# Moving the loads of q, k and v from SyncE's queue to GpSimd's in a fused attention and feed-forward kernel

## The chip, the cores and the metric

The kernel runs on one core of a Trainium2 chip. Five engines work side by side: TensorE (PE; its weight loads are shown as PEld), VectorE (DVE), ScalarE (ACT), GpSimd (POOL) and SyncE (SP), which computes nothing and only issues transfers and semaphores. Each engine runs its own instructions in order; transfers are carried out by 16 DMA engines. The metric is the time of one execution on the device in microseconds (us).

## The reference

For 8 batches of 8 heads, 576 tokens and 64 features (everything float32):

```python
scores = scale * np.matmul(q, k.transpose(0, 1, 3, 2))          # scale = 1/8
thresh = np.max(scores, axis=-1, keepdims=True) - tau            # tau = 0.02
scores = np.where(scores >= thresh, scores, -1000000000.0)
attn = np.exp(scores - np.max(scores, axis=-1, keepdims=True))
attn = attn / (np.sum(attn, axis=-1, keepdims=True) + 1e-09)
x = np.matmul(attn, v)            # heads side by side: 4608 tokens x 512
h = x @ w_in                      # 512 x 2048
out = np.maximum(0.01 * h, h) @ w_out                            # 2048 x 512
```

A weight of the attention is kept only where its score lies within `tau` of the row's largest.

## The kernel before

The work is cut into 72 **periods**: 128 queries of one batch by four heads (64 periods), and for each pair of batches two periods for the last 64 tokens of all heads (8 periods). A pair of batches makes 18 periods. A Python loop over `n` writes out all instructions in the order in which each engine is to run them; no scheduler moves them. Iteration `n` holds the scores of period `n`, the transposed transfer of the weights of period `n - 1`, the product with v of period `n - 2` (`PV_LAG = 2`), and a share of the feed-forward layers for groups of 128 tokens whose attention is done.

In one iteration the engines run, each in this order:

- PE: the score matmuls (L296) into one PSUM tile `sc` for four tiles of 128x576; transposes of the split q and k (`turn(keys)`, L186); a transpose that spreads the reciprocals (L401); four calls of `layer2` (L470), two of `layer1` (L457), and between them `pv` (L417), the weights times v. `l1q` holds what `layer1` is still to do. In odd iterations its second call takes the `x` that DVE has just written in the same iteration.
- DVE: copies of `sc` to SBUF with the row minimum (L332, four times; between the first two, half of the transposed q or k, L249), the reciprocals of the period before (L376), the thresholds `th` (L347: 128x4 values, SBUF to SBUF), `x` out of `pv` (L436), and the weights of three tiles (`weights`, L369: compare with the threshold, multiply, sum).
- ACT: three exponentials (`exp_plain`, L358), the leaky relu (L460), `by` (L407), every second period the output tile `osb` (L478), and `exp_steep` (L363, L364), which makes the weights of the fourth tile on ACT alone with a Prelu and an Exp.
- POOL: splits of q or k into a high and a low half (L160, L167, L171) ahead of their transposes, casts of v (L113, L119), one widening copy for each batch's keys (`widen_keys`, L253), and a one-instruction score signal (L325). The first work of POOL in an iteration waits for DVE's last weights of the period before (`behind_masks`). In iterations 0 to 2 POOL also issues the loads of `w_in` and `w_out` (L123, L127), four of 512 KB each.
- SP: `turn_w` (L380), one DMA that transposes the weights `w` of the period before into `wT`; then that iteration's loads of q, k and v; then the stores of finished output tiles.

The score signal orders two halves of the score matmuls that share a PSUM bank: it waits for a matmul of one row half, and the first matmul of the piece `a12` of the other row half waits for it. It sits on ACT for periods 0 to 2 and on POOL after that.

Loads are given to iterations by a table, `loads_at`. A main load of q, k or v (`load_main` L75, `load_v` L99) has 512 KB for four heads; tails (L93, L106) come as two transfers of 64 rows each. The first two batches' q and k are loaded in part by `load_part` (L86, 128 KB). From iteration 5 on, most iterations issue one to four loads; the last are issued in iteration 60. A load is used two or more periods after its issue.

SP's part of an iteration in the code:

```python
        elif before and st:
            turn_w(before)
        landed = [f() for f in loads_at.get(n, [])]
        while stores:
            store()
```

and the signal:

```python
            if (h, x) == (1, b12) and i == 2:
                signal = (nc.scalar if st.n < 3 else nc.gpsimd).nop()
```

The last group of tokens, (B-1, 3), is evacuated by ACT and DVE together (L475, L476) and stored by two queues (L492).

Of the kernel before, what the change touches and what calls it, by code (L numbers as in the profile page):

```python
# [12 lines left out]
AF = mybir.ActivationFunctionType  # L13
# [20 lines left out]
def kernel(  # L34
# [10 lines left out]
    nc = tc.nc  # L45
# [21 lines left out]
    raws, tails, vraws, vtails = {}, {}, {}, {}  # L67
    SRC = {"q": q, "k": k}

    def load_main(b, s, which):  # L70
        if (b, s, which) in MIXED:
            return [load_part(b, s, which, t=t) for t in range(4)][0]
        t = sb.tile([128, 4, 256], FP32, tag="raw", bufs=4, name="raw")
        raws[b, s, which] = t
        return nc.sync.dma_start(  # L75
            out=t[:, :, :], in_=SRC[which][b, ds(4 * s, 4), 0:MAIN, :].rearrange("h (p t) d -> p h (t d)", t=4))


# [2 lines left out]
    def load_part(b, s, which, h=None, t=None, eng=None):  # L81
        if (b, s, which) not in raws:
            raws[b, s, which] = sb.tile([128, 4, 4, 64], FP32, tag="raw", bufs=4, name="raw")
        src = SRC[which][b, ds(4 * s, 4), 0:MAIN, :].rearrange("h (p t) d -> p h t d", t=4)
        dst = raws[b, s, which]
        return (eng or nc.sync).dma_start(out=dst[:, :, h, :] if t is None else dst[:, t, :, :],  # L86
                                          in_=src[:, h, :, :] if t is None else src[:, :, t, :])

    def load_tails(b, which, engines=None):
        t = sb.tile([128, 2, 2, 64], FP32, tag="rawt", bufs=4, name="rawt")  # L90
        src = SRC[which][b, :, MAIN:S, :].rearrange("(u sh) p d -> u p sh d", u=2)
        for u, eng in enumerate(engines or (nc.sync, nc.sync)):
            eng.dma_start(out=t[ds(64 * u, 64), :, :, :].rearrange("p s h d -> p (s h) d"), in_=src[u])  # L93
        tails[b, which] = t

    def load_v(b, s):
        t = sb.tile([128, 4, 256], FP32, tag="vraw", bufs=2, name="vraw")
        vraws[b, s] = t
        return nc.sync.dma_start(  # L99
            out=t[:, :, :], in_=v[b, ds(4 * s, 4), 0:MAIN, :].rearrange("h (p t) d -> p h (t d)", t=4))  # L100

    def load_vtails(b):
        t = sb.tile([128, NP, 64], FP32, tag="vrawt", bufs=1, name="vrawt")
        src = v[b, :, MAIN:S, :].rearrange("(r h) p d -> h p r d", h=2)
        for h in range(2):
            nc.sync.dma_start(out=t[ds(64 * h, 64), :, :], in_=src[h])  # L106
        vtails[b] = t

    def cast_v(b, p, copy=None):
# [191 lines left out]
    def scores(st):  # L301

        st.mn = sb.tile([128, 4], FP32, tag="mn", bufs=2, name="mn")
        st.th = sb.tile([128, 4], FP32, tag="th", bufs=2, name="th")
        st.s, st.e = {}, {}
        (a00, a01), (b01, b00) = pieces(0, 0), pieces(0, 1)
        (a11, a12), (b12, b11) = pieces(1, 0), pieces(1, 1)
        todo = [[(0, a00), (0, a01), (1, a11), (1, a12)], [(1, b12), (1, b11), (0, b01), (0, b00)]]
        if st.n < 2:

            todo[1] = todo[1][2:] + todo[1][:2]
        todo = [[(c, x, i) for c, x in row for i in range(3)] for row in todo]
        at_, signal, first = [0, 0], None, None
        while todo[0] or todo[1]:
            h = 1 if not todo[0] or (todo[1] and at_[1] < at_[0]) else 0
            c, x, i = todo[h].pop(0)
            at_[h] += x[1]
            for mm in product(st, c, h, x, i):
                if first is not None:
                    tc.declare_no_dep(mm.ins, first.ins, reason="other banks")  # L320
                if (h, x) == (0, a12) and i == 0:
                    tc.add_manual_dep(mm.ins, signal.ins.name, BEHIND, reason="the row halves share a bank")
                last = mm
            if (h, x) == (1, b12) and i == 2:
                signal = (nc.scalar if st.n < 3 else nc.gpsimd).nop()  # L325
                tc.add_manual_dep(signal.ins, last.ins.name, BEHIND, reason="the row halves share a bank")
            if (h, x) == (0, a11) and i == 2:
                first = copy_min(st, 0)
# [135 lines left out]
    def layer2():  # L464
        g, r = l2q.pop(0)
        if r == 0:
            g.o = ps.tile([128, 512], FP32, tag="o", bufs=1, name="o")
        for j in (2 * r, 2 * r + 1):
            for c in range(2):
                nc.tensor.matmul(out=g.o[ds(64 * c, 64), :], lhsT=g.g[:, j, ds(64 * c, 64)],  # L470
                                 rhs=w_out16[:, j, :], start=(j == 0), stop=(j == 15), skip_group_check=True)
        if r == 7:
            g.out = sb.tile([128, 512], FP32, tag="osb", bufs=3, name="osb")
            if g.where == (B - 1, 3):
                nc.scalar.activation(out=g.out[:, 0:256], in_=g.o[:, 0:256], func=AF.Copy, bias=0.0, scale=1.0)  # L475
                nc.vector.tensor_copy(out=g.out[:, 256:512], in_=g.o[:, 256:512])  # L476
            else:
                nc.scalar.activation(out=g.out[:, :], in_=g.o[:, :], func=AF.Copy, bias=0.0, scale=1.0)  # L478
            stores.append(g)

    def store():
        g = stores.pop(0)
        b, m = g.where
        if m is None:
            for u in range(2):
                nc.sync.dma_start(out=out[ds((b + u) * S + MAIN, 64), :], in_=g.out[ds(64 * u, 64), :])
        else:
            rows = out[ds(b * S, MAIN), :].rearrange("(p t) f -> p t f", t=4)
            parts = (nc.scalar, nc.sync) if g.where == (B - 1, 3) else (nc.sync,)
            for i, eng in enumerate(parts):  # L490
                f = ts(i, 512 // len(parts))
                eng.dma_start(out=rows[:, m, f], in_=g.out[:, f])  # L492


    loads_at, turns_at, early32, late32, split_at_, pool_at = {}, {}, {}, {}, {}, {}
# [119 lines left out]
    n = 0  # L615
    while n < N + PV_LAG or l1q or pending or l2q or stores:
        st = periods[n] if n < N else None
        before = periods[n - 1] if 1 <= n <= N else None
        due = periods[n - PV_LAG] if PV_LAG <= n < N + PV_LAG else None
        here = before and before.n < 3  # L620
        keys, now32, late = turns_at.get(n, []), early32.get(n, []), late32.get(n)


# [30 lines left out]
        for key in keys:  # L654
            if key[1:] == ("t", "k"):
                widen_keys(key[0])
        if n < 4:
            idle((16, 10, 8, 4)[n], spare("o"))
        if here:
# [2 lines left out]
                turn_w_here(before, 0, 8, o)  # L662
        elif before and st:
            turn_w(before)
        landed = [f() for f in loads_at.get(n, [])]
        while stores:
            store()
        if n == 0:
# [12 lines left out]
        for half in range(2):  # L681
            if half == 1 and n == 3:
                exp_steep(st, 3)
            for _ in range(2):
                if l2q:
                    layer2()
            if l1q:
                layer1()
            elif n >= N:
                settle()  # L690
            if half == 0:
                if st:
                    exp_plain(st, 1)
                    exp_plain(st, 2)
                if here:
                    take_w(before, 0, 8, o, on_act)
                if late:
                    turn32(late)
                    take_high(late)
                if n == N:  # L700

                    before.wt = sb.tile([128, 2, 9, 128], FP16, tag="wT", bufs=4, name="wT")
                    free = [(sc[:, ts(i, 512)].bitcast(FP16), 8 * i, m) for i, m in enumerate((8, 8, 2))]
                    for o, first, m in free:
                        turn_w_here(before, first, m, o)
                if due and n <= N:
                    if n != 3:
                        pv(due)
                    evacuate(due)
                if n == N:  # L710
                    a, *more = [take_w(before, first, m, o[:, 0 : 128 * m], on_dve if first else on_act)
                                for o, first, m in free]
                    for x in more:
                        tc.declare_no_dep(x.ins, a.ins, reason="other banks")
            elif st and n != 3:
                exp_steep(st, 3)
        if here:
            o = ps.tile([128, 512], FP16, tag="o", bufs=1, name="wp")
            turn_w_here(before, 8, 4, o)
        for i in range(3 if st else 0):  # L720
            weights(st, i)
            if late and i == 0:
                take_low(late)
            if here and i == 1:
                take_w(before, 8, 4, o, on_dve)
# [34 lines left out]
```

## Time and profile before

| | |
|---|---|
| median of 3 runs | 484.28 us (483.44 to 484.53) |
| the profiled execution | 484.76 us, its span 482.9 us |
| PE busy | 465.4 us, 96% of the span |
| DVE, ACT, POOL busy | 434.8, 418.4, 190.9 us |
| granted TensorE clock | 1.00 |
| HBM read, written | 36.70 MB, 9.44 MB |
| transposed transfers `wT<-w` on SP | 68; from issue to landing 4.5 / 6.2 / 9.4 us (least, median, most) |
| main loads on SP, issue to landing | 4.9 to 5.6 us |

The span runs from the first to the last instruction of the trace; the execution's time has 1.9 us around it. [...] The chain that ended last is made up of PE by 75% and of the transfers `wT<-w` by 12%.

### The profile page before, as it was taken

What the parts mean: (1) busy time and instruction counts of PE and PEld (TensorE: products, weight loads), DVE (VectorE), ACT (ScalarE), POOL (GpSimd) and SP (SyncE); (2) the same over time, 40 slices, a digit from 0 to 9 for tenths busy, and PEclk for the clock granted to TensorE, in tenths of its full rate; (3) what the DMA queues carried; (4) which work ended last, traced back from release to release, by engine and by line L of the source; (5) the groups of instructions that cost most, each with busy time, mean ns of one, the idle gap of its engine ahead of it and who ended that gap; (6) DMA issues with size and microseconds to landing.
All of it is one profiled execution on the core that took longest, in us unless ns stands there. A gap on an engine that the chain in (4) does not pass through costs nothing.

```text
span 482.9 us, 25246 instructions
## 1 busy us (share of the span) xinstructions
PE 465.4 (96%) x10858; PEld 378.9 (78%) x10858; DVE 434.8 (90%) x1315; ACT 418.4 (87%) x777; POOL 190.9 (40%) x313
## 2 busy tenths in 40 slices
PE   7779999999999999999999999999999999999996
PEld 5567788888887788888887788888878888777785
DVE  4999989999999999999999999999998999999940
ACT  3888889999998899998998999999998899988862
POOL 2544436543554444353454554353454444000000
PEclk9999999999999999999999999999999999999999
DMA  9999998898979989799989969898989988657851
GB/s 177 237 210 218 193 224 167 160 192 194 190 165 207 182 165 188 151 177 192 193 167 215 209 142 189 150 194 181 203 167 184 215 168 135 124 122 123 122 96 45
DMA packets 216480, 83.68 MB, mean 173 GB/s; under 512 B 186032, under 2 KB 211888, under 8 KB 216368
## 3 DMA queue, kind: packets, MB, share of 16 engines
q1 hardware_dynamic: 210672, 77.42, 83.2%
q0 software_dynamic: 4224, 4.19, 5.3%
q8 instruction: 85, 1.39, 1.2%
q10 hardware_dynamic: 1472, 0.46, 0.4%
q14 instruction: 27, 0.22, 0.1%
HBM read 36.70 MB, written 9.44 MB: 96 GB/s over the span
## 4 chain that ended last, share of the span: by engine, by line
PE 75%; DMA 13%; ACT 6%; DVE 2%; issue 2%; SPq 0%; POOL 0%; ACTq 0%; POOLq 0%; DVEq 0%
PE hp L457 22%; PE o L470 22%; PE sc L296 18%; DMA wT<-w 12%; PE pv L417 8%; PE tp L401 3%; PE tp L186 2%; ACT e L358 1%; DVE w L369 1%; ACT w L364 1%; DMA vrawt<-in_v_dram 1%; ACT s L363 1%; ACT wT L393 1%; DMA raw<-in_k_dram 1%; DVE s L332 1%
## 5 line engine op out<-in xcount | busy, mean ns | idle before, releaser
L332 DVE TENSOR_SCALAR_CACHE_REDUCE s<-sc 128x576 f32<-128x576 f32 x288 | 205.4, 753 | 15.9 <-PE sc L296 15.8
L457 PEld LDWEIGHTS <-win 128*64 128x64 f16 x4608 | 146.8, 110 | 29.1 <-issue 1.4
L369 DVE SCALAR_TENSOR_TENSOR w<-s,th,e 128x576 f16<-128x576 f32 x216 | 166.3, 816 | 0.2
L358 ACT ACTIVATE e<-s,mn 128x576 f16<-128x576 f32 x216 | 159.7, 778 | 0.0
L470 PE MATMUL o<-wout,g 128*64 128x512 f16 x1152 | 149.3, 379 | 0.5 <-issue 0.5
L457 PE MATMUL hp<-x,win 128*64 128x128 f16 x4096 | 136.7, 219 | 0.3 <-DVE kT L249 0.3
L460 ACT ACTIVATE g<-hp 128x512 f16<-128x512 f32 x144 | 86.2, 598 | 44.5 <-PE hp L457 44.5
L296 PE MATMUL sc<-kT,qT 64*128 64x384 f16 (+7 forms) x1920 | 119.6, 284 | 0.7 <-DVE kT L239 0.7
L296 PEld LDWEIGHTS <-qT 64*128 64x128 f16 (+1 forms) x1920 | 90.3, 97 | 16.4 <-issue 1.4
L160 POOL TENSOR_SCALAR scaled<-raw 128x512 f32<-128x512 f32 x53 | 32.8, 620 | 169.0 <-DVE w L369 158.5
L470 PEld LDWEIGHTS <-g 128*64 128x64 f16 x1152 | 58.9, 110 | 28.6 <-ACT g L460 0.3
L171 POOL TENSOR_TENSOR half<-scaled,half 128x512 f16<-128x512 f32 (+1 forms) x68 | 71.8, 1056 | 5.8
L417 PE MATMUL pv<-wT,v 128*64 128x128 f16 (+1 forms) x1600 | 53.3, 215 | 4.9 <-DMA wT<-w 3.7
L364 ACT ACTIVATE w<-s,minus_tau 128x576 f16<-128x576 f32 x72 | 55.8, 775 | 2.3
L363 ACT ACTIVATE s<-s,th 128x576 f32<-128x576 f32 x72 | 55.2, 767 | 0.0
L417 PEld LDWEIGHTS <-v 128*64 128x64 f16 x1600 | 45.8, 110 | 6.6 <-PE hp L457 4.5
L167 POOL CAST half<-scaled 128x512 f16<-128x512 f32 (+1 forms) x68 | 38.4, 564 | 4.4
L436 DVE TENSOR_TENSOR x<-pv,by 128x256 f16<-128x256 f32 x64 | 27.1, 424 | 9.4 <-PE pv L417 5.7
L407 ACT COPY by<-tp 128x256 f16<-128x256 f16 x72 | 26.8, 372 | 3.4 <-PE tp L388 3.4
L186 PEld LDWEIGHTS <-half 64*128 64x128 f16 x968 | 24.4, 95 | 2.4 <-issue 1.5
L186 PE MATMUL tp<-ident,half 64*128 64x64 f16 x968 | 24.4, 190 | 0.0
L113 POOL CAST v<-vraw 128x256 f16<-128x256 f32 x64 | 24.1, 410 | 0.0
(58 smaller groups left out, 311.9 us busy)
## 6 DMA issues: line engine op xcount, KB each, us to landing
vraw<-in_v_dram SPq DMA_DIRECT2D x16, 512.0 KB, 5.2
out_dram<-osb SPq DMA_DIRECT2D x31, 256.0 KB, 5.0
raw<-in_q_dram SPq DMA_DIRECT2D x13, 512.0 KB, 5.6
raw<-in_k_dram SPq DMA_DIRECT2D x13, 512.0 KB, 4.9
win<-in_moe_w_in_dram POOLq DMA_DIRECT2D x4, 512.0 KB, 11.2
wout<-in_moe_w_out_dram POOLq DMA_DIRECT2D x4, 512.0 KB, 14.9
raw<-in_q_dram SPq DMA_DIRECT2D x12, 128.0 KB, 3.9
raw<-in_k_dram SPq DMA_DIRECT2D x10, 128.0 KB, 4.2
```

The source lines that it names most:

```text
L171: nc.gpsimd.tensor_tensor(out=halves[key][:, 1, 0:n, :, :], in0=scaled.pop(key)[:, 0:n, :, :], in1=halves[key][:, 0, 0:n, :, :], op=AX.sub ...
L186: nc.tensor.transpose(tps[key][r][:, x, t, :], half[rows, x, t, :, :].rearrange("p h d -> p (h d)"), ident[rows, rows])
L296: yield nc.tensor.matmul(out=o, lhsT=lhs, rhs=turned[st.b, "k"][rows, kx, pair, ds(key0, n)], start=(i == 0), stop=(i == 2), skip_group_ch ...
L332: return nc.vector.tensor_scalar(out=st.s[TILES[n]][:, :], in0=sc[:, ds(PLACE[TILES[n]], 576)], scalar1=-1.0 / UNIT, scalar2=None, op0=AX. ...
L358: nc.scalar.activation(out=st.e[t][:, :], in_=st.s[t][:, :], func=AF.Exp, bias=st.mn[:, n : n + 1], scale=-1.0)
L363: nc.scalar.activation(out=z, in_=z, func=AF.Prelu, bias=st.th[:, n : n + 1], scale=-1.0, alpha=1e20)
L364: nc.scalar.activation(out=w_of(st, t), in_=z, func=AF.Exp, bias=minus_tau[:, :], scale=1.0, accum_out=st.sum[:, c, h : h + 1])
L369: st.last = nc.vector.scalar_tensor_tensor(out=w_of(st, t), in0=st.s[t][:, :], scalar=st.th[:, n : n + 1], in1=st.e[t][:, :], op0=AX.is_le ...
L417: nc.tensor.matmul(out=st.pv[ds(64 * h, 64), c, ts(u, n)], lhsT=v16[st.b % 2][:, pair, blk, :], rhs=st.wt[:, c, blk - (blk > 4), ts(u, n)] ...
L457: nc.tensor.matmul(out=hp[ds(64 * c, 64), jj, :], lhsT=w_in16[:, i, ds(128 * (4 * u + jj) + 64 * c, 64)], rhs=g.x[:, i, :], start=(i == 0) ...
L460: nc.scalar.activation(out=g.g[:, ds(4 * u, 4), :], in_=hp[:, :, :], func=AF.Prelu, bias=0.0, scale=1.0, alpha=0.01)
L470: nc.tensor.matmul(out=g.o[ds(64 * c, 64), :], lhsT=g.g[:, j, ds(64 * c, 64)], rhs=w_out16[:, j, :], start=(j == 0), stop=(j == 15), skip_ ...
```

## The change

Four edits. From iteration 5 on, the loads of q, k and v are issued by GpSimd instead of SyncE, behind the splits, casts and widening copies of the iteration; before that they stay where they were. The score signal sits on ACT for periods 0 to 2, on POOL for 3 to 5 and on SP from 6 on. In period 1 the third tile is made by `exp_steep` on ACT like the fourth, so DVE makes the weights of two tiles and ACT runs one plain exponential less and one Prelu and Exp more. The last group is evacuated and stored by row halves (64 rows of 512 columns) instead of column halves, and the two copies are declared independent. The transfers' addresses and sizes are otherwise the same: 84 DMA instructions move from SP to POOL.

```diff
+    loader = [nc.sync]
+
     def load_main(b, s, which):
...
-        return nc.sync.dma_start(
+        return loader[0].dma_start(
...
     def load_part(b, s, which, h=None, t=None, eng=None):
...
-        return (eng or nc.sync).dma_start(out=dst[:, :, h, :] if t is None else dst[:, t, :, :],
+        return (eng or loader[0]).dma_start(out=dst[:, :, h, :] if t is None else dst[:, t, :, :],
...
     def load_tails(b, which, engines=None):
-        for u, eng in enumerate(engines or (nc.sync, nc.sync)):
+        for u, eng in enumerate(engines or (loader[0], loader[0])):
...
     def load_v(b, s):
-        return nc.sync.dma_start(
+        return loader[0].dma_start(
...
     def load_vtails(b):
-            nc.sync.dma_start(out=t[ds(64 * h, 64), :, :], in_=src[h])
+            loader[0].dma_start(out=t[ds(64 * h, 64), :, :], in_=src[h])
...
             if (h, x) == (1, b12) and i == 2:
-                signal = (nc.scalar if st.n < 3 else nc.gpsimd).nop()
+                signal = (nc.scalar if st.n < 3 else nc.gpsimd if st.n < 6 else nc.sync).nop()
...
             if g.where == (B - 1, 3):
-                nc.scalar.activation(out=g.out[:, 0:256], in_=g.o[:, 0:256], func=AF.Copy, bias=0.0, scale=1.0)
-                nc.vector.tensor_copy(out=g.out[:, 256:512], in_=g.o[:, 256:512])
+                a = nc.scalar.activation(out=g.out[0:64, :], in_=g.o[0:64, :], func=AF.Copy, bias=0.0, scale=1.0)
+                x = nc.vector.tensor_copy(out=g.out[64:128, :], in_=g.o[64:128, :])
+                tc.declare_no_dep(x.ins, a.ins, reason="other rows")
...
             for i, eng in enumerate(parts):
-                f = ts(i, 512 // len(parts))
-                eng.dma_start(out=rows[:, m, f], in_=g.out[:, f])
+                n = 128 // len(parts)
+                eng.dma_start(out=rows[ts(i, n), m, :], in_=g.out[ts(i, n), :])
...
+        plain = 2 if n == 1 else 3
...
             if key[1:] == ("t", "k"):
                 widen_keys(key[0])
+        if n >= 5:
+
+            loader[0] = nc.gpsimd
+            for f in loads_at.get(n, []):
+                f()
...
         elif before and st:
             turn_w(before)
-        landed = [f() for f in loads_at.get(n, [])]
+        if n < 5:
+            for f in loads_at.get(n, []):
+                f()
         while stores:
             store()
...
                 if st:
-                    exp_plain(st, 1)
-                    exp_plain(st, 2)
+                    for i in range(1, plain):
+                        exp_plain(st, i)
...
             elif st and n != 3:
-                exp_steep(st, 3)
+                for i in range(plain, 4):
+                    exp_steep(st, i)
...
-        for i in range(3 if st else 0):
+        for i in range(plain if st else 0):
             weights(st, i)
```

## The prediction

> **What bounds the kernel now.** I read the shares first, then the waits, then single periods.
>
> From part 1 of the page:
>
> ```profile
> PE 465.4 (96%) x10858; PEld 378.9 (78%) x10858; DVE 434.8 (90%) x1315; ACT 418.4 (87%) x777; POOL 190.9 (40%) x313
> ```
>
> PE (TensorE) works in 96% of the span, POOL (GpSimd) in 40%. The edit moves work off SP, which computes nothing, onto POOL, so the question is what PE still waits for. The list of waits (engine, its line, what it waited for: us in total, times, longest):
>
> ```profile
> DVE s L332 <- PE sc L296: 15.8, 62, 0.4
> ...
> PE pv L417 <- DMA wT<-w: 3.7, 7, 0.8
> ```
>
> The first row says that VectorE (DVE) has about 0.25 us to spare in a period. The second is the one large wait of PE that the moved queue can touch: seven times `pv` stood for the transposed weights. Two undisturbed periods and a stalled one, from the table of windows (stretch, length, busy us of each engine, granted clock, DMA share, GB/s):
>
> ```profile
> 102.93:109.04 6.11, 6.11 (x148) 5.01 (x145) 5.88 (x19) 5.85 (x11) 2.40 (x3) 1.00 0.99 211
> 109.04:115.15 6.11, 6.11 (x148) 5.02 (x144) 5.88 (x19) 5.47 (x10) 2.40 (x3) 1.00 0.81 164
> 145.77:152.60 6.83, 6.31 (x150) 5.20 (x146) 6.06 (x19) 5.47 (x10) 2.86 (x7) 1.00 1.02 219
> ```
>
> An undisturbed period is 6.11 us, all of it PE, with DVE 0.23 behind. The clock is at full speed, so it plays no part. Period 21 lost 0.72. [...]
>
> ```profile
> 140.36 0.55 SPq L99 DMA_DIRECT2D vraw<-in_v_dram  x1
> 140.96 0.49 SPq L492 DMA_DIRECT2D out_dram<-osb  x1
> 141.95 4.41 SPq L380 DMA_TRANSPOSE wT<-w  x1
> 146.41 0.58 SPq L75 DMA_DIRECT2D raw<-in_k_dram  x1
> 147.09 2.13 SPq L106 DMA_DIRECT2D vrawt<-in_v_dram  x2
> 149.38 3.26 SPq L380 DMA_TRANSPOSE wT<-w  x1
> ```
>
> The turn of 141.95 was issued 1.6 us behind a 512 KB load and 1 us behind a store; its issue took 4.41 and its data landed at 150.02, 8.07 later, with `pv` waiting. The three loads behind it (2.71) then kept SP until 149.22, so the next turn started 3.6 us after its period's scores instead of 2.29. The tile of these transfers shows how common that is:
>
> ```profile
> L380 SPq DMA_TRANSPOSE wT<-w x68: 2473/3183/5870, 38.5 to 458.2; - x68
> ...
> DMA to landing us min/median/max: 4.5/6.2/9.4
> ```
>
> `pv` needs the data some 7.5 us after issue: the median turn has 1.3 us to spare, and those issued right behind loads have nothing.
>
> **Turns without loads ahead of them: −2.9 us.** Stalled periods that the edit can reach are 21 (6.83), 23 (6.85), 33 (6.56), 39 (7.12) and 41 (6.79): above 6.11 that is 0.72 + 0.74 + 0.45 + 1.01 + 0.68 = 3.6, less 0.11 twice, since periods 22 and 40 then took 6.00: 3.4. In the quiet stretch without loads (iterations 63 to 70) turns land in 4.6 to 6.6, all in time. In the changed kernel loads leave POOL about 4.3 us after the scores begin, that is 2 us after the turn's issue and well before the next turn, and no turn queues behind them. A load can now run beside the end of the turn just issued, though. If it delayed that landing by 0.5 us, the parts above their slack over the 30 such turns sum to 0.5. I take −3.4 + 0.5 = −2.9 (ends −3.4 and 0).
>
> **Period 6: +0.8 us.** Turns of periods 3 and 4 lie behind transfers that the edit leaves (0.37 and 0.70 of wait in iterations 5 and 6). But four q loads of 128 KB, issued on SP at 51.45 when turn 4 was out, now leave POOL from about 48.7, beside that turn (issued 48.11, landed 54.97, needed at once). They hold 0.5 MB; at the 0.2 MB per us of the page's GB/s row that is 2.5 us of transfer. Ends 0 and +2.5; I take a third, since the first packets of a turn come 1.2 us after its issue and so lead those of the loads by about a microsecond.
>
> **What the loads cost on POOL.** No 512 KB load from POOL is in the steady part; the nearest rows are the weight loads, of the same size: 0.75 us for each. POOL has 3.5 us free in a period, so its own time costs nothing. But the weight loads show a neighbour that suffers:
>
> ```profile
> 26.33 1.49 POOL L127 DMA_DIRECT2D wout<-in_moe_w_out_dram  x2
> ```
>
> ```profile
> 27.25 0.17 DVE L376 RECIPROCAL rec<-sum 128x4 f16<-128x4 f32 x1
> 27.36 0.46 DVE L347 TENSOR_SCALAR th<-mn 128x4 f32<-128x4 f32 x1
> ```
>
> `th`, DVE's 128x4 threshold, has a median of 0.17 us. Here it took 0.46, ending with the second of the two POOL instructions, inside which it began by 0.29; at 19.76 it took 0.49 and began 0.26 inside. `rec` was not held. [...]
>
> Behind `th` on DVE stands `x` (L436), which `layer1` takes at once in odd iterations (0.05 to 0.15 us of slack); in even ones DVE's 0.23 of idle time takes back part. So the cost hangs on where the loads fall. The first operation of POOL in a period starts with DVE's last weights, and `th` comes 3.3 us later. POOL's work ahead of the loads takes 2.54 (one split: the load of 0.75 is just over), 3.0 to 3.1, 3.23 (split and two casts), or about 4 (behind `th`). Period 20 has the third kind, with 0.74 of casts there and `th` at their heels:
>
> ```profile
> 143.37 0.74 POOL L113 CAST v<-vraw 128x256 f16<-128x256 f32 x2
> ```
>
> ```profile
> 144.18 0.17 DVE L347 TENSOR_SCALAR th<-mn 128x4 f32<-128x4 f32 x1
> 144.26 0.42 DVE L436 TENSOR_TENSOR x<-pv,by 128x256 f16<-128x256 f32 x1
> ```
>
> The load would begin at about 144.11, `th` 0.07 later. The rows show `th` held when it came 0.26 into such an instruction, and none that came earlier. I let it pass under 0.2. Then it is held in odd periods 13, 21, 31, 39 and 49 by 0.23, 0.27, 0.22, 0.27, 0.22 = 1.2, less 0.05 of slack each: **+1.0** (ends +0.5 and +6.0, the upper one in the first rival).
>
> **Edits that cost little.** The score signal waits on SP behind the turn's issue: from 2.29 to 5.0 in a median period, up to 8.2 with the longest (the store adds 0.5); it is needed at 6.11 + 1.15 = 7.26. Behind it stands only the next turn, due later. Cover is the 2 us between; without it one period loses up to 1. I take 0. The third tile of period 1 takes 0.81 + 0.08 from DVE and puts 0.77 + 0.78 + 0.19 for one exp of 0.78 on ACT; iteration 5's `pv` waits for a turn landing at 47.91 whatever comes before: 0 (−0.15 to +0.3). At the end the osb copies ran one behind the other (ACT 0.38 at 479.09, DVE 0.42 at 479.51). Side by side, over half the rows and twice the columns, about 0.6 and 0.69: ready at 479.78 in place of 479.94: −0.15.
>
> **Sum.** −2.9 + 0.8 + 1.0 + 0 + 0 − 0.15 = −1.25, from 484.76 (the span of 482.9 and 1.9 around it) to 483.5. That run lay 0.48 above the median 484.28; on that scale: **483.0**. Its own range is 481.3 to 484.6.
>
> **Rival 1: the loads hold `th` (slower).** The deciding point is whether a POOL load holds `th` from its very start, as the widening copy L253 did: `th` began 13 ns behind it and took 0.63. Then the periods of 3.23 count in full. Odd ones: 7, 13, 17, 21, 31, 35, 39, 49, 53, 57, by 0.42 + 0.23 + 0.49 + 0.50 + 0.22 + 0.50 + 0.50 + 0.22 + 0.49 + 0.50 = 4.1, less 0.05 to 0.15 each; nine even ones (20, 22, 24, 26 and those 18 later, 58) hand on up to 0.27 each: 4.0 to 6.0, I take 4.5. −2.9 + 0.8 + 4.5 − 0.15 = +2.25: 486.5, up to 488. [...]
>
> **Rival 2: the load starves the turn beside it (slower).** Turn 3, issued at 38.51 while the weight loads of POOL's queue still ran, took 9.4 to land. If each load delays its own period's turn by 1.2 us, the parts above slack sum to about 4 in place of 0.5 (1.0 gives 2.2; 1.5 already 8.4): −3.4 + 4 + 0.8 + 1.0 − 0.15 = +2.25: 486.5, with a tail to 491. Against it: a load's first packets come 1 to 1.7 us after its start, when most of the turn is through.
>
> **Rival 3: the queue is not the cause.** The bytes stay the same, DMA share is 0.8 to 1 with loads, and if landings spread by that alone, turns stay as late: 0 + 0.8 + 1.0 − 0.15 = +1.65: 485.9. [...]
>
> **Chances.** Forecast 0.52 (0.08 of it ends within 0.2%), rival 1 0.22 (0.04 within), rival 2 0.16 (0.02), rival 3 0.10 (0.02). 0.2% is 1 us, about what a measurement of this kernel can tell from no change. Faster 0.44, same 0.16, slower 0.40. The range runs from the forecast's lower end to past rivals 1 and 3, leaving out the tail of rival 2: 481.2 to 489.0.
>
> **What would show it.** Right: turns landing within 7 us, the wait of `pv` for `wT` under 1.5 us in total, periods 21 to 41 at 6.11 to 6.3, a few `th` of 0.4 to 0.6. Rival 1: twenty or more long `th`, each with `hp` waiting behind `x` in odd periods. Rival 2: turn landings above 7.5 in periods with loads. Wrong altogether: PE waiting for the signal's semaphore, or splits waiting for late loads.

## Result and the profile after

The changed kernel took 510.96 us (median of 5 runs, 507.11 to 511.36) against 484.28 us: 1.054 times as long, with an interval of 1.049 to 1.058. The forecast was 483.0, its range 481.2 to 489.0, so both the sign and the range were wrong. The profiled execution has a span of 509.6 us, 26.7 more than before.

First the page of the changed kernel: busy time, then the DMA queues (packets, MB, share of the 16 engines' span).

```profile
PE 472.8 (93%) x10858; PEld 383.6 (75%) x10858; DVE 434.8 (85%) x1313; ACT 420.0 (82%) x779; POOL 246.7 (48%) x394
...
q1 hardware_dynamic: 178080, 54.87, 62.4%
q0 software_dynamic: 11024, 26.74, 21.6%
```

The loads went to the software queue as planned: q0 carries 26.74 MB, and POOL runs 81 instructions more (394 against 313), so 81 loads moved and not 84. VectorE works exactly as long as before, PE 7.4 us longer, and the span grew by 26.7: PE waits. The list of waits says for what (total us, times, longest):

```profile
PEld L419 <- issue: 19.0, 9, 5.6
PE pv L419 <- DMA wT<-w: 18.4, 10, 5.5
```

`pv` (L417, now L419) stood 18.4 us for the turn's data where it had stood 3.7. The row of PEld goes with the same stalls, seen from the weight loads, so the two are not added. The tile of the turns:

```profile
L382 SPq DMA_TRANSPOSE wT<-w x68: 2441/2953/7001, 38.2 to 484.3; - x68
...
DMA to landing us min/median/max: 4.6/6.6/14.3
```

The median turn is issued in less time (2.95 us against 3.18): SyncE did get shorter work, which is what the forecast counted on. But the data lands later (6.6 against 6.2), and the worst turn takes 14.3. Of 68 turns 21 took over 7.5 us, before 8. Set against the kernel before, period by period (from VectorE's first copy of one period to that of the next), 18.6 of the 26.7 us lie in three periods: 21 (+7.8), 39 (+6.0) and 57 (+4.8), 18 apart; 5 and 6 cost 3.1, and 16 has 1.9. The windows of period 21 and of two undisturbed ones (columns as before):

```profile
151.06:165.67 14.61, 8.66 (x149) 6.62 (x146) 7.20 (x22) 5.59 (x10) 4.45 (x10) 0.77 1.07 158
178.38:184.50 6.12, 6.12 (x149) 5.02 (x146) 5.81 (x19) 5.85 (x11) 4.75 (x8) 1.00 0.60 132
184.50:190.61 6.11, 6.11 (x149) 5.01 (x146) 5.88 (x19) 5.47 (x10) 4.62 (x8) 1.00 0.94 133
```

The undisturbed periods are still 6.11: nothing is lost where the turn is in time. Period 21 lasts 14.61, and the granted clock is 0.77 there. What led to it, on POOL's timeline and in the chain that ended last:

```profile
144.64 0.78 POOL L101 DMA_DIRECT2D vraw<-in_v_dram  x1
...
149.34 0.81 POOL L77 DMA_DIRECT2D raw<-in_k_dram  x1
150.16 1.24 POOL L108 DMA_DIRECT2D vrawt<-in_v_dram  x2
```

```profile
147.24 13.67 DMA wT<-w
160.91 0.14 issue
161.05 1.28 PE pv L419 x20
```

A load of v was issued 2.6 us ahead of the turn of 147.24, one of k 2.1 us behind it and two tails of v after that. That turn took 13.67 us. Ahead of it on SyncE's queue lay only a store of 144.37, which landed at 147.62; the four loads landed between 152.74 and 160.70, the turn at 160.91. In those 13.67 us the 16 engines carried 0.88 MB of SyncE's queue and 1.16 MB of GpSimd's side by side.

### The profile page after: what moved, and what is told of

It is laid out like the page before. It is cut to its first block, busy times and chain, and to the rows that moved or that the text cites. A ratio compares the mean times of both kernels' runs of the same rounds, so it can differ in the third digit from the quotient of the medians.

```text
span 509.6 us, 25224 instructions
## 1 busy us (share of the span) xinstructions
PE 472.8 (93%) x10858; PEld 383.6 (75%) x10858; DVE 434.8 (85%) x1313; ACT 420.0 (82%) x779; POOL 246.7 (48%) x394
## 3 DMA queue, kind: packets, MB, share of 16 engines
q0 software_dynamic: 11024, 26.74, 21.6%
## 4 chain that ended last, share of the span: by engine, by line
PE 70%; DMA 18%; ACT 6%; issue 2%; DVE 2%; SPq 0%; ACTq 0%; DVEq 0%
PE hp L459 20%; PE o L472 20%; DMA wT<-w 17%; PE sc L298 17%; PE pv L419 8%; PE tp L403 3%; PE tp L188 2%; ACT e L360 1%; ACT s L365 1%; ACT wT L395 1%; ACT w L366 1%; DMA raw<-in_k_dram 1%; DVE w L371 1%; DVE s L334 1%; ACT g L462 0%
## 5 line engine op out<-in xcount | busy, mean ns | idle before, releaser
L459 PEld LDWEIGHTS <-win 128*64 128x64 f16 x4608 | 149.5, 111 | 29.2 <-issue 1.9
L472 PE MATMUL o<-wout,g 128*64 128x512 f16 x1152 | 150.9, 383 | 0.0
L459 PE MATMUL hp<-x,win 128*64 128x128 f16 x4096 | 139.0, 221 | 0.3 <-DVE kT L251 0.3
L298 PE MATMUL sc<-kT,qT 64*128 64x384 f16 (+7 forms) x1920 | 120.8, 284 | 2.8 <-ACTq L327 1.1
L298 PEld LDWEIGHTS <-qT 64*128 64x128 f16 (+1 forms) x1920 | 90.3, 97 | 20.0 <-ACTq L327 2.0
L419 PE MATMUL pv<-wT,v 128*64 128x128 f16 (+1 forms) x1600 | 54.3, 217 | 22.4 <-DMA wT<-w 18.4
L419 PEld LDWEIGHTS <-v 128*64 128x64 f16 x1600 | 46.5, 112 | 24.9 <-issue 19.0
L334 DVE DVE_READ_ACCUMULATOR s<-sc 128x1 f32 x288 | 24.2, 84 | 0.0
```

What stands on the lines that cost most here:

```text
L298: yield nc.tensor.matmul(out=o, lhsT=lhs, rhs=turned[st.b, "k"][rows, kx, pair, ds(key0, n)], start=(i == 0), stop=(i == 2), skip_group_ch ...
L334: return nc.vector.tensor_scalar(out=st.s[TILES[n]][:, :], in0=sc[:, ds(PLACE[TILES[n]], 576)], scalar1=-1.0 / UNIT, scalar2=None, op0=AX. ...
L419: nc.tensor.matmul(out=st.pv[ds(64 * h, 64), c, ts(u, n)], lhsT=v16[st.b % 2][:, pair, blk, :], rhs=st.wt[:, c, blk - (blk > 4), ts(u, n)] ...
L459: nc.tensor.matmul(out=hp[ds(64 * c, 64), jj, :], lhsT=w_in16[:, i, ds(128 * (4 * u + jj) + 64 * c, 64)], rhs=g.x[:, i, :], start=(i == 0) ...
```

## Experiments

Times are medians, ratios stand against the kernel before in the same session (484.95, 485.05 and 485.58 us there). "Over" is the span of the profiled execution less the 482.9 of before. Single executions of one kernel spread by 3 to 7 us where the turns are disturbed, and single periods by several us from profile to profile. e8 to e12 and e14 ran once each.

**e1: loads back on SyncE, the rest of the change kept.**

```diff
-        if n >= 5:
-            loader[0] = nc.gpsimd
-            for f in loads_at.get(n, []):
-                f()
...
-        if n < 5:
-            for f in loads_at.get(n, []):
-                f()
+        for f in loads_at.get(n, []):
+            f()
```

> The changed kernel with one edit undone: the loads go back to SyncE, behind the turn; signal on SyncE, the third tile of period 1 and the row halves at the end stay. Theories of the 26.7 us: (Q) a load on a second queue shares the DMA engines with a turn and delays it; (S) the signal, now behind the turn's issue on SyncE, delays the scores. By Q the time comes back to 484 (483.5 to 485), turns land in 4.5/6.2/9.4 as before. By S at least 5 us stay: above 489.

500.75 us, ratio 1.030 (1.025 to 1.036), where Q had 484 and S above 489: here the signal decides. The turns did come back, as Q had it: four took over 7.5 us, and `pv` stood 2.6 us for them instead of 18.4. But the signal now stands behind loads on SyncE:

```profile
PEld L298 <- SPq L327: 18.2, 14, 3.0
...
PE sc L298 <- SPq L327: 14.0, 13, 2.7
```

PE stood 14.0 us for SyncE's signal (L327), up to 2.7 us at a time, of 16.2 over; the row of PEld has the same stalls from the weight loads. So the signal can stand on SyncE only if the loads do not; the two edits belong together, and in the changed kernel what it still costs is small: its rows there are

```profile
  ACTq L327: 3.1, 4
  SPq L327: 2.8, 5
```

under the scores (L298). These rows add PE and its weight loads: the 2.8 us on SyncE are three stalls, in two of which PE itself stood, 0.9 us in all. The ACT row belongs to periods 0 to 2.

**e2: the loads' queue alone.**

```diff
-    signal = (nc.scalar if st.n < 3 else nc.gpsimd if st.n < 6 else nc.sync).nop()
+    signal = (nc.scalar if st.n < 3 else nc.gpsimd).nop()
...
-        plain = 2 if n == 1 else 3
+        plain = 3
```

and the column halves at the end, as before.

> The kernel before with one edit alone: loads from period 5 on GpSimd's queue; the signal stays on GpSimd from period 3, now behind the loads. By Q the time is that of the changed kernel, 507 to 512, with the great stalls in periods 21, 39 and 57. By S it is under 500, since the signal no longer waits for a turn's issue.

504.55 us, ratio 1.041 (1.036 to 1.047); 20.3 over: above S's 500 and a little under Q's 507. No signal on SyncE, and three quarters of the loss are there; the other 6 us of the changed kernel no run takes apart. Period 6 lost 5.8, period 57 6.2, period 21 only 1.3: which turn is hit changes, that some are hit does not.

**e3 and e5: the same loads, released later.** POOL's loads wait for VectorE's first weights of the period; e5 also has the signal on POOL and period 1 and the end as before.

```diff
         for i in range(plain if st else 0):
             weights(st, i)
+            if i == 0 and n >= 5:
+                loader[0] = nc.gpsimd
+                for f in loads_at.get(n, []):
+                    for mm in f():
+                        behind_masks(mm, st)
```

> The changed kernel with the loads on GpSimd held until VectorE has made the first weights of the period, about 1.4 us later (5.8 us after the scores begin in place of 4.3), when most of the turn just issued is through and the next is 2.6 us off. If what hurts is that the loads leave too early, beside that turn (T), the time comes back to 484 to 488. If a load from this queue delays any turn that it meets (Q), it now meets the next one: 500 to 515.

490.91 us, ratio 1.012 (1.006 to 1.017): above T's 488, and far below Q's 500. So the loads do not simply delay the next turn in place of this one.

> As e3 (loads on GpSimd behind VectorE's first weights), but with the score signal back on GpSimd and period 1 and the end as before: of the change only the loads' queue is left, with the later release. e3 was 6.0 us over before in its profile; 0.7 of it at the end, some 5.9 where PE waited for the signal or a turn. If the release decides (T) and the signal was the rest, 484 to 487. If the queue itself costs (Q), 489 or more. A cost of its own: in iterations with three or four loads GpSimd issues until 7.9 to 8.3 us after the scores begin, and the next signal, due at 7.26, stands behind it: up to 1 us in each of some six periods.

487.52 us, ratio 1.007 (1.004 to 1.010), just above the band of T and below Q's 489. Same queue, same bytes, and 17 of the 20 us are gone. PE's first two rows of waits for e5:

```profile
PE pv L418 <- DMA wT<-w: 3.8, 5, 1.4
PE wp L389 <- ACT wT L394: 2.8, 3, 1.4
```

3.8 us for the turns is what the kernel before has (3.7). The feared wait for the signal behind the loads is there and is small: five stalls, 2.0 us for the weight loads and 0.5 for PE itself.

**e6: an intermediate release,** by VectorE's `x` instead of its first weights; otherwise e5.

```diff
                     evacuate(due)
+                    if n >= 5:
+                        loader[0] = nc.gpsimd
+                        for f in loads_at.get(n, []):
+                            for mm in f():
+                                tc.add_manual_dep(mm.ins, due.evacuated.ins.name, BEHIND, ...)
```

> As e5, but the loads are released by VectorE's x, 5.0 us after the scores begin: 0.7 us later than in the changed kernel, 0.8 us earlier than in e5. If the load does harm by meeting the turn just issued (T), it lies between e2 (20 us over) and e5, nearer to e5: 487 to 494, and the great stalls of periods 6, 21, 39, 57 are under 3 us. If the release plays no part, it is at e2's 503 to 506.

491.40 us (median of three executions; a fourth took 499.23), ratio 1.013 (1.010 to 1.017): between e2 and e5, as T has it, but the great stalls were not all under 3: periods 6 and 57 lost 5.2 and 4.3. Measured from the turn's issue to the load's (median of POOL's loads), the three releases give a row: 2.1 us, 504.6; 3.45 us, 491.4; 4.0 us, 487.5. The kernel before issues its loads 3.55 us behind the turn, on the turn's own queue, at 485.

**e4: a second hardware queue.** The loads from period 5 are issued by ScalarE.

```diff
                     for i in range(1, plain):
                         exp_plain(st, i)
+                        if i == 1 and n >= 5:
+                            loader[0] = nc.scalar
+                            for f in loads_at.get(n, []):
+                                f()
```

> The changed kernel with the loads from period 5 issued by ScalarE behind its second exponential: a second hardware queue in place of the software queue, at about the same time. Each issue takes ScalarE some 0.5 to 0.6 us. If any second queue delays the turns (Q), great stalls stay in periods 21, 39 and 57 and the time is 500 to 515. If it is the software queue with its packets of 4096 bytes (P: 159 ns each against 46 ns for 1024 on SyncE's queue), the turns land in under 8 us and the time is 484 to 492, what is lost being ScalarE's time.

504.81 us, ratio 1.043 (1.038 to 1.049). 20 turns took over 7.5 us, 21 in the changed kernel. This speaks for Q, but not cleanly: the loads left 1.7 us behind the turn, earlier than in e2, and PE also waited for ScalarE, which paid 0.37 us for a 512 KB load. Periods 21, 39 and 57 did not stall (-0.9 to +0.3; period 6 lost 4.3). The probes e9 to e11 take the two apart.

**e7: the loads on SyncE, spread.** The kernel before with two times in its table changed.

```diff
-  rows, t_at, v_at = (E - 3, E - 2, E + 2, E + 3), (E + 1, E + 6), (E + 1, E + 4, E + 2)
+  rows, t_at, v_at = (E - 3, E - 2, E + 2, E + 3), (E, E + 6), (E + 1, E + 4, E)
```

> The kernel before, all loads on SyncE, with two kinds of loads of the odd batches moved: the tails of k from iteration 19 to 18 and those of v from 20 to 18 (and 18 and 36 later), where nothing was loaded. If the old stalls in periods 21, 23, 39, 41 came of loads bunched on SyncE ahead of the turn (as the forecast had it), three quarters of their 2.9 us go, 482 to 483.2. If they come of the DMA engines' load, 484 to 485.

483.08 us (12 runs), ratio 0.9965 (0.9945 to 0.9985). This one beats both kernels, if by little. The wait is what went:

```profile
PE pv L417 <- DMA wT<-w: 1.4, 2, 0.8
```

1.4 us in place of 3.7. The time is inside the forecast's band, so it is in line with reading the old stalls as loads bunched ahead of the turn; the cure for them is on SyncE's own queue. Period by period it is less clean: 21, 23 and 41 fell to 6.11, but 39, the longest, took 7.72 where it had 7.12, and with the old table the wait was as low as 1.8 us in one other profile (e10, ahead of its extra loads).

**e8: the small edits** (loads and signal as before; third tile of period 1 on ScalarE, row halves at the end).

> The changed kernel with loads on SyncE behind the turn as before and the signal on GpSimd as before: what is left is the third tile of period 1 on ScalarE and the row halves at the end. From the profiles so far: periods 1 and 2 together -0.2, period 5 as before or 0.8 longer, the last stretch 0.65 longer; in all 484.5 to 486 us.

485.13 us, one execution; 0.5 over. Period 1 is 1.5 shorter and period 2 1.25 longer (its scores wait for the signal on ScalarE, which does more in period 1); the last stretch is 0.64 longer, as in every kernel with the row halves.

**e9 to e12, e14: one load by itself.** The kernel before, with one more load in iterations 63, 65, 67 and 69, which load nothing.

```diff
             exp_plain(st, 0)
+            if n in (63, 65, 67, 69):
+                extra = sb.tile([128, 4, 256], FP32, tag="raw", bufs=4, name="extra")
+                mm = nc.gpsimd.dma_start(out=extra[:, :, :], in_=q[n % 8, ds(0, 4), 0:MAIN, :]...)
+                tc.add_manual_dep(mm.ins, st.second.ins.name, BEHIND, ...)
```

e10 has `nc.scalar` there, e11 a float16 tile, e12 stands behind the first weights, e14 has two loads.

> A measurement of one load by itself: the kernel before, and in iterations 63, 65, 67 and 69, where nothing is loaded, one more 512 KB load of q into a free buffer (nobody reads it) from GpSimd's queue, released by VectorE's second copy, 2.6 us after the scores begin, just behind the issue of the turn. The turns of iterations 64, 66, 68 and 70 are the controls (4.6 to 6.6 us in the kernel before). By Q and by P the turns issued in the four iterations land 1.3 to 4 us later than the controls; by a theory that only loads in number do harm, under 1 us later.

> The same four extra loads with the same release, from ScalarE's hardware queue: packets of 1024 bytes. By Q (any second queue) the four turns are delayed as in e9, within 0.7 us; by P (the software queue and its 4096-byte packets) by less than half of that.

> The same four extra loads from GpSimd's queue as in e9, but into a float16 buffer, so that packets have 1024 bytes as those of the weight loads, in the same software queue. If the size of the packets does the harm, the four turns are delayed by less than half of e9; if the queue or the meeting does, as in e9 or more (four times the packets, 98 ns each as in the weight loads).

> The same four extra loads as e9 from GpSimd's queue, released by VectorE's first weights, 5.8 us after the scores begin. By T the turn issued in the iteration is not delayed (4.6 to 6.6 as the controls), and the next one by under 1 us. By a theory that the queue itself slows turns wherever it works, one of the two turns is delayed as in e9.

> The probe e9 with two loads of 512 KB in a row beside each of the four turns in place of one. One load made them land 2.4 us later (7.8 on average against 5.4). If the delay is the time of the transfer that the turn meets (proportional), two make it 4 to 5.5 us: landings of 9.5 to 11. If a bunch feeds on itself (bunch), the four land more than 6.5 us later, at 12 or above, or the next turn is over 2 us late too.

The turns of the chain in e9 (start, us from issue to landing):

```profile
410.02 7.54 DMA wT<-w
...
422.34 8.64 DMA wT<-w
...
435.83 7.53 DMA wT<-w
...
448.13 7.46 DMA wT<-w
```

In the kernel before the same four turns took 5.05, 4.56, 6.28 and 5.69 and were not on the chain. The whole table, four turns each:

| | turn beside the load, mean us | the next turn, mean us |
|---|---|---|
| before (no load) | 5.4 | 5.8 |
| e9 GpSimd, 4096-byte packets | 7.8 | 6.3 |
| e10 ScalarE, 1024-byte packets | 7.2 | 6.1 |
| e11 GpSimd, cast to float16 | 7.5 | 6.1 |
| e12 GpSimd, released 5.8 us after the scores begin | 5.4 | 6.4 |
| e14 GpSimd, two loads | 8.7 | 7.5 |

`st.second` is VectorE's second copy of the period. One load beside a turn makes it land 2.4 us later; from another queue (+1.8) or with other packets (+2.1) nearly as much, so P falls (four turns each scatter by about 1). The same load 2.7 us later (3.6 us behind the turn's issue in place of 0.9) does the turn no harm and costs the next one 0.6: T stands, and of Q what is left is that a load of either second queue delays the turn if it leaves early enough. No run has a load that early on SyncE's own queue, where a turn's issue alone takes 2.4 us or more. Two loads delay this turn by 3.3 and the next by 1.7: more harm, but less than twice to the first, so neither of e14's bounds was met; a bunch does not feed on itself in four isolated turns.

What is late differs with the queue. A turn has 2304 packets of 256 bytes. The queues' packets in e9 in the first 4.3 us behind the issue of the turn of 422.34 (packets, MB, share of the 16 engines' time):

```profile
q1 hardware_dynamic: 2304, 0.59, 72.3%
q0 software_dynamic: 16, 0.07, 10.5%
```

All of the turn's packets had begun by then, as they had for the same turn without the load (422.80 in the kernel before, landed after 4.56), and 16 of the load's; the landing came at 8.64. Over the four turns the last packet ended 4.5 us behind the issue before, 4.6 in e9, 4.5 in e11 and e14: with loads on GpSimd's queue the packets are in time and the landing alone is late. In e10 the turn's packets themselves ended at 6.3 on average, and the landing followed 1.0 later, as it does without a load (0.9).

So the move to GpSimd's queue saved a turn 0.2 us of issue at the median (2.95 against 3.18) and cost it 2.4 us of landing where it met a load (e9).

**e13: the changed kernel with e7's table.**

> The changed kernel with e7's table of loads: the tails of k and of v of the odd batches leave in iteration 18 (and 18, 36 later) in place of 19 and 20, so that no iteration with main loads has more than one transfer. Periods 21, 39 and 57 cost the changed kernel 7.8 + 6.0 + 4.8 = 18.6 us. If those three come of several loads in a row beside the turns (bunch), they fall under 2 us each and the time to 492 to 498. If one main load beside a turn can do it alone (single), they stay or move to other periods: 503 to 511.

499.79 us, ratio 1.028 (1.022 to 1.033): 11 us less than the changed kernel. Periods 21, 39 and 57 now stand at -0.7, +1.2 and 0, as "bunch" has it, though e2 with the old table lost only 1.3 and 1.2 in 21 and 39, so part of this can be chance. The time lies above the band of "bunch": periods 6 and 8 lost 6.2 and 4.2 in the profiled execution (at 505.38 the slowest of its four). These follow bunches too, which e7's table leaves as they are: four q loads of 128 KB left from 48.56 to 50.86 beside the turn of 48.22, which took 10.86, and two loads of 512 KB at 66.49 and 67.31 beside the turn of 66.11, which took 11.17. So the largest stalls stand behind bunches; the other 10 of the 20.7 over are small losses in many periods.

## Why the prediction was wrong, step by step

**Turns without loads ahead of them: -2.9 us.** This step failed. Its gain was real: SyncE's issues became shorter, and e7 shows about 2 us to be had by taking loads from in front of turns. Its price, half a microsecond for the load "beside the end of the turn just issued", was mis-sized: one meeting costs the turn 2.4 us (e9), not 0.5. The step's own sum shows how steep that is: with 2.0 us added to each of the 30 landings, what exceeds each turn's slack sums to some 18 us (28 with 2.4), against 0.5 us for 0.5. The measured loss of the loads alone is 20.3 (e2); that 18 is close to it is luck, since most of the loss stands in a few turns that met several loads and not in thirty equal delays. The argument against rival 2 was that most of the turn is through when the load's first packets come. For the packets that is so (e9), but the landing still came 2.4 us later: with loads from GpSimd's queue a turn is not through when its packets are.

Part of the 3.4 us that the step wanted back was not steady either. In e9 and e12, the kernel before up to iteration 62, two of its five periods, 23 and 33, are 0.6 to 0.7 and 0.45 shorter than in the profile of before: those stalls did not come back, so a single profile had them by chance.

**Rival 2** was the right mechanism, a load beside the turn, with the wrong size. It had a delay of 1.2 us for each turn, 486.5, and named 8.4 us for 1.5; it ended at 491 and had a chance of 0.16. It should have used the one row that it cited, a turn of 9.4 us beside weight loads, as its price.

**Rival 1 and the +1.0 for `th`.** Too large: `th` of over 0.2 us sum to 2.0 us above the median in the changed kernel, 1.8 before. What the loads add to `th` plays no part in the 26.7 us. No run shows a load of q, k or v holding `th` from the load's start, from which rival 1's +4.5 is added up: in the changed kernel the 22 `th` that began up to 0.23 us into such a load took 0.17, and the five that were held began 0.31 to 0.53 into one and took 0.24 to 0.43, 0.8 us in all above the median. One that began 0.12 into a weight load took 0.65.

**Rival 3** was wrong: the landings did change with the queue and with when the loads leave it, for the worse (a median of 6.6 us and at most 14.3, against 6.2 and 9.4).

**Period 6: +0.8.** Right place, mis-sized: periods 5 and 6 cost 3.1, and period 6 alone 5.8 in e2 and 6.2 in e13.

**The signal: 0.** Nearly right: PE stood 0.9 us for it, in two stalls. The step named the condition (a long issue ahead of it), and the turns' issues reached 7.0 us.

**The end: -0.15.** Wrong sign. The copies did run side by side, and the last store was issued 0.73 us after the first copy began in place of 0.87, as forecast:

```profile
505.12 0.59 ACT L477 ACTIVATE osb<-o 64x512 f32<-64x512 f32 x1 [1.15 <-PE o L472]
505.12 0.69 DVE L478 COPY osb<-o 64x512 f32<-64x512 f32 x1 [10.04 <-PE o L472]
```

but the stores of 64 rows land after 2.50 and 2.68 us where the column halves took 1.95 and 1.96, so the last stretch is 0.66 longer. The step had costed the copies and not the transfers behind them.

**The third tile of period 1: 0.** Right; what period 1 gains, period 2 gives back.

Open is why a turn that meets several transfers can take 13 us, and what a landing waits for when its packets are done: between 151 and 152 the 16 engines were busy by 0.05, with the turn and four loads unfinished. What the queues waited for there no run shows.

## What to carry to other kernels

Here the busy queue also set when its transfers left: behind the turn on SyncE's queue the 512 KB loads left 2.7 to 5.2 us after it, from GpSimd's queue at a median of 2.0. The one queue did not keep transfers apart: in the kernel before, 493 of the 512 packets of the load of 146.41 began before the turn of 141.95, ahead of it on the same queue, had landed. It made the load leave later, and the later it left the less it cost (e2, e6, e5: 2.1, 3.45 and 4.0 us behind the turn, 504.6, 491.4 and 487.5). Before moving a load to an idle queue, find the time at which it will then leave and the transfer that it will meet there, and price that meeting by the slack of each transfer: by the estimate above 0.5 us on each of the 30 turns costs 0.5 us and 2.0 us costs some 18. If loads must run beside such a transfer, try releasing them by a later event, as e5 does, or spreading them over the iterations that load nothing, as e7 does. Here the later release only won back what the move had cost (e5 is still 2.5 us behind the kernel before); the spreading on SyncE's own queue was the gain.

## What was not expected of the hardware

The size of the packets hardly mattered: from GpSimd's queue 4096 bytes, at a median of 159 ns each, delayed a turn by 2.4 us and 1024 bytes, at 98 ns, by 2.1; from ScalarE's queue 1024 bytes, at 46 ns, did so by 1.8.

In period 21 of the changed kernel the stalled PE lost time twice. Two windows of 1 us in it (columns as before, the granted clock third from the end):

```profile
158.00:159.00 1.00, 0.00 (x0) 0.00 (x0) 0.00 (x0) 0.00 (x0) 0.00 (x0) 0.95 2.83 136
...
163.00:164.00 1.00, 1.00 (x10) 0.56 (x8) 1.00 (x3) 0.00 (x0) 0.00 (x0) 0.50 0.95 259
```

After 3.4 us without matmuls (from 155.55 to 158.91) the clock fell to 0.50, and it came back 4.7 us after they had begun again at 161.05, so PE was busy for 8.66 us in that period instead of about 6.3: 2.4 us on top of the 5.9 that it stood idle. The first of these delays is not fixed here: in the trace's two other stalls with a slow clock it fell 2.1 us into a pause of 4.5 (from 276.26), and 1.2 us after a pause of 3.0 was over (at 400.04), while it came back 4.5 and 4.6 us after the matmuls had begun again.
